# A routed MoE kernel: a late transfer on another queue, expert 0 in tiles of 416 and 384 tokens, and another order of copies and products at the end

## The chip, the cores and the metric

The kernel runs on one core of one Trainium2 chip. The core has five engines that run on their own and wait for each other by semaphores: TensorE (PE in the profile; PEld is its loading of weights), VectorE (DVE), ScalarE (ACT), GpSimd (POOL) and SyncE (SP), which here only issues transfers. The metric is device time in microseconds, the median over runs. The kernel before took 938.18 us (three runs, 937.0 to 938.84).

## The reference, cut to what matters

Two blocks follow each other. The first is attention with a polynomial sketch, over 4 batches, 4 heads, 1088 positions and 32 dimensions; its output becomes x, with one row for each of the 4352 tokens. The second routes every token to all 8 experts, with weights from 8 rounds of Sinkhorn scaling.

```
q_p, k_p = phi(q), phi(k)                 # phi: products of two projections, 64 features
num = q_p @ (k_p^T v);  den = q_p . sum(k_p) + 1e-6
x = (num / den), as (B*S, H*D) = (4352, 128)
P = exp(x @ w_gate - max)
8 times: P /= row sums; P /= column sums; P *= N / E
out = sum over e of P[:, e] * (relu(x @ w1[e]) @ w2[e])     # F = 1024
```

The column sums go over all tokens, so the routing can't begin before the last token's x is there. An expert's two products don't need the routing: only its weight in the sum does.

## The kernel before, in words

x is held transposed, as `xT`, 128 features by 4352 tokens. For each token the experts' products are by far the largest work. They are cut into groups, listed in `groups`: first token, tile width, number of tiles, experts, and whether the weights of the routing are multiplied into x first. While attention and routing still run, the plain groups are computed: expert 0 over all tokens but with its result stored unweighted in `kept`, and expert 1 over 1280 of them. The other groups are weighted, and take the experts that remain, on pieces of 256 tokens.

A plain group has two tiles. Its second product uses a scheme with seven products of half blocks in place of eight (`seven`), so VectorE forms differences of the relu outputs (L911, in `two`), and the sums come out in four PSUM banks. Each group goes through four blocks of four steps. A step is one first product with w1 (L894), its relu on ScalarE (L898), and second products (L1067) of a block that began eight steps earlier (`LAG`). When a group's banks are full, `part_of_seven` unloads them: ScalarE copies (L729 to L744) and VectorE adds (L720 and L723). The next group can write to a bank only when that bank has been read; bank 0 is free after L723 on `kept`, the fourth bank after L723 on `w`.

Attention and routing are written as generators (`attention`, `routing`) and are mixed with these steps by `fill(n)`: it advances the expert work by about n units, where a step with tiles of 480 tokens is one unit and a step with n tokens n/480. The order of TensorE and VectorE is thus written out by hand in this stretch; ScalarE's is set by a scheduler.

Attention of batches 1 to 3 runs in three thirds. For each, `tops` makes the products (L454), `over` divides and turns the result (L473), and `take_over` moves it into `xT` through DRAM: one transfer out (L478), then one for each of four heads (L480). For batch 3 this is done in two pieces, after the second and after the third third, both on GpSimd's queue. Once everything is there, `logits` multiplies x by w_gate (L488), VectorE turns the result (L497), and the Sinkhorn rounds alternate between VectorE (L587 to L603) and one small product on TensorE (L597). At the end the weights go to DRAM as `pT` (L609), and come back spread over partitions as `xe`, which GpSimd multiplies with x (L663).

The last group has two tiles of 256 tokens. Its last two blocks are written out with their products in an order of their own (`last_products`): of the last eight blocks, the products that go to bank 1 are held back and fill TensorE at the end, while the other three banks are unloaded. `last_part` does that: banks are finished in the order 3, 0, 2, 1, and copies (L772 to L782), adds (L764), transposes (L699) and stores (L852) follow.

Of the kernel before, what the change touches and what calls it, by code (L numbers as in the profile page):

```python
# [50 lines left out]
def kernel(  # L51
# [12 lines left out]
    nc = tc.nc  # L64
# [62 lines left out]
    W9 = 9 * 32  # L127
# [159 lines left out]
    def transpose_q(b, lo=0, hi=S):  # L287
        to = kT if b == 1 else qT
        nc.vector.transpose(out=to[:, lo:hi], in_=loaded["q", b].rearrange("p a d -> p (a d)")[:, lo:hi])
# [35 lines left out]
    def keys_sums(b):  # L325

        kp, vx = products.pop(b), v_slots[b % 2]
        pv = bank()[:, 0:128].rearrange("p (i c d) -> p i c d", i=2, c=2)

        slots = [slice(h, H + 1, H - h) for h in range(H)]  # L330

        for t in range(NT + 1):
            n = P if t < NT else 64
            for h in range(H):
                i, s = divmod(h, 2)
                nc.tensor.matmul(pv[64 * s:64 * (s + 1), i], kp[0:n, H * t + h].rearrange("p i j -> p (i j)"),  # L336
                                 vx[0:n, slots[h], t, :], start=(t == 0 and i == 0), stop=(t == NT and i == 1),
                                 tile_position=(0, 64 * s))
        sums_of[b] = pv
# [3 lines left out]
    def keys_kept(b):  # L343
        pv = sums_of.pop(b)
        for s in range(2):
            sl = slice(64 * s, 64 * (s + 1))
            if b:
                x, y = kvs[b % 2][sl, :, s, :], pv[sl].rearrange("p i c d -> p i (c d)")[:, :, 0:D + 1]
            else:
                x, y = kvz[sl, :, :, s, :], pv[sl].rearrange("p i c d -> p c i d")  # L350
            if s:
                nc.vector.tensor_copy(x, y)
            else:
                nc.scalar.copy(x, y)
# [55 lines left out]
    def queries_ab(b):  # L410
        qa = dram.tile([H * R, 2, 2, 2 * W9], F32, name=f"qa{b}")
        qb = dram.tile([2, R, 2 * R, 2, 2 * W9], F32, name=f"qb{b}")
        ab = wk.tile([P, 3, 192], F32, tag="qab", name="qab", bufs=1)
        x = (kT if b == 1 else qT).rearrange("p (h q c t s) -> p h c t q s", h=2, q=2, c=3, t=3)
        for cs in ((0, 1), (2,)):
            pq = bank()[:, 0:192 * len(cs)].rearrange("p (c n) -> p c n", n=192)
            for i, c in enumerate(cs):
                for s in range(2):
                    nc.tensor.matmul(pq[64 * s:64 * (s + 1), i].rearrange("p (t q s) -> p t q s", t=3, q=2),
                                     wdq.rearrange("p n f -> p (n f)"), x[:, s, c], start=True, stop=True,  # L420
                                     tile_position=(0, 64 * s))
            nc.scalar.copy(ab[:, cs[0]:cs[-1] + 1], pq)
        abf = ab.rearrange("p c n -> p (c n)")
        for s in range(2):
            x = abf[64 * s:64 * s + 32].unsqueeze(1).to_broadcast([32, 2, 2 * W9])
            nc.sync.dma_start(out=qa[:, :, s], in_=x)
        for s in range(2):
            for h in range(2):
                x = abf[64 * s + 32 + h:64 * (s + 1):2].unsqueeze(1).to_broadcast([2 * R, R, 2 * W9])
                nc.sync.dma_start(out=qb[h, :, :, s].rearrange("i f n -> f i n"), in_=x)  # L430
        queries[b] = qa, qb
# [11 lines left out]
    def times(b, c):  # L443
        ph = third(phs[b % 2], c)
        nc.vector.tensor_tensor(ph, ph, third(rb, c), op=Alu.mult)

    def tops(b, c):

        pn = bank()[:, 0:3 * H * (D + 1)].rearrange("p (t h d) -> p t h d", t=3, h=H)
        ph = third(phs[b % 2], c)  # L450
        for t in range(3):
            for i in range(2):
                for s in range(2):
                    nc.tensor.matmul(pn[64 * s:64 * (s + 1), t, 2 * i:2 * i + 2].rearrange("p h d -> p (h d)"),  # L454
                                     ph[:, i, s, 64 * t:64 * (t + 1)], kvs[b % 2][:, i].rearrange("p h d -> p (h d)"),
                                     start=(t == 0 and i == 0), stop=False, tile_position=(0, 64 * s))
        for s in range(2):
            nc.tensor.matmul(pn[64 * s:64 * (s + 1), :, :, D], ones[:, 0:64], eps, start=False, stop=True,
                             tile_position=(0, 64 * s))
        queries[b, c] = pn  # L460

    turned = {}
# [9 lines left out]
            turned[b] = wk.tile([P, H, W9], F32, tag="xt", name="xt", bufs=1)  # L472
        nc.vector.transpose(out=turned[b][:, :, 96 * c:96 * (c + 1)].rearrange("p h (t s) -> p h t s", t=3), in_=xs)  # L473

    def take_over(b, lo, hi):

        xd = dram.tile([P, H, hi - lo], F32, name=f"xd{b}{lo}")
        nc.gpsimd.dma_start(out=xd, in_=turned[b][:, :, lo:hi])  # L478
        for h in range(H):
            nc.gpsimd.dma_start(  # L480
                out=xT[32 * h:32 * (h + 1), b * S:b * S + 4 * W9].rearrange("d (f n) -> d f n", f=4)[:, :, lo:hi],
                in_=xd.rearrange("(f d) h n -> h d f n", f=4)[h])

# [15 lines left out]
    def attention(b):  # L499


        follows = b + 1 < B
        keys_sums(b)
        times(b, 0)
        yield
        keys_kept(b)
        times(b, 1)
        tops(b, 0)
        if b == 1:
            transpose_q(2)  # L510
        yield
        times(b, 2)
        if b == 1:
            queries_ab(2)
            repeat_a(2)
        if follows:
            repeat_b(b + 1)
        over(b, 0)
        tops(b, 1)
        yield  # L520
        over(b, 1)
        if b + 1 == B:
            take_over(b, 0, 192)
        yield
        tops(b, 2)
        if follows:
            transpose_k(b + 1)
        if b + 2 < B:
            load_k(b + 2)
            load_v(b + 2)  # L530
        yield
        over(b, 2)
        if b + 1 < B:
            take_over(b, 0, W9)
        else:
            take_over(b, 192, W9)
        if follows:
            keys_ab(b + 1)
            yield
            keys_products(b + 1, 0)  # L540
            if b == 1:
                transpose_q(3)
            yield
            keys_products(b + 1, 1)
            if b == 1:
                queries_ab(3)
                repeat_a(3)
            yield
            keys_products(b + 1, 2)
            yield  # L550
# [11 lines left out]
    def routing():  # L562
# [45 lines left out]
        for b in (1, 0, 2, 3):  # L608
# [8 lines left out]
    lower, upper = slice(0, H2), slice(H2, P)  # L617
# [3 lines left out]


    groups = [(0, 256, 2, [0], False), (512, 288, 2, [0], False), (0, 256, 2, [1], False),
              *((1088 + 960 * i, 480, 2, [0], False) for i in range(3)), (3968, 192, 2, [0], False),
              (512, 384, 2, [1], False)]
    PLAIN = len(groups)
    for lo in (1280, 512, 2048, 2816, 3584):
# [83 lines left out]
    def room(tag, n=NMAX):  # L711
        return keep.tile([P, NMAX], F32, tag=tag, name=tag)[:, 0:n]
# [44 lines left out]
    def last_part(g, k):  # L757


        lo, n, *_ = groups[g]  # L760
        s0, s1, s2, s3 = sums[g]

        def add(out, a, b):
            nc.vector.tensor_tensor(out, a, b, op=Alu.add)  # L764

        own = parts.setdefault(g, {})
        if not own:
            own.update(y=[pools[0].tile([P, NT3], F32, name=f"y{t}", bufs=1)[:, 0:n] for t in range(2)],
                       **{a: room(a, n) for a in "zwxfr"})
        (y1, y2), z, w, x, f, r = (own[a] for a in "yzwxfr")  # L770
        if k == 3:
            nc.scalar.copy(r[upper], s3[lower])  # L772
            add(w[upper], s3[upper], r[upper])
        elif k == 0:
            nc.scalar.copy(z[upper], s0[lower])
            nc.scalar.copy(f[lower], s0[upper])
            add(x[upper], z[upper], w[upper])
            add(z[upper], x[upper], s0[upper])
            add(z[lower], s0[lower], f[lower])
            nc.scalar.copy(x[lower], s0[lower])  # L780
        elif k == 2:
            nc.scalar.copy(r[lower], s2[upper])  # L782
            add(y2[upper], z[upper], s2[upper])
            add(z[lower], z[lower], s2[lower])
            add(y2[lower], z[lower], r[lower])
            add(x[upper], x[upper], s2[upper])
            put(y2, lo + n, n, (nc.sync, nc.scalar))
        else:
            add(y1, s1, x)
            put(y1, lo, n, (nc.sync, nc.scalar))  # L790
# [220 lines left out]
    held = []  # L1011

    def last_products():

        k = len(blocks) - 2
        one, two_ = ([[(b, p) for p in ps] for ps in seven(b)] for b in (k, k + 1))
        return one + held[:3] + two_ + held[3:]

    def kept_to_sums(g):

# [205 lines left out]
```

## Time and profile before

| what | us |
| --- | --- |
| median of three runs | 938.18 |
| span of the profiled execution | 933.0 |
| TensorE busy | 914.5 |
| VectorE busy | 693.6 |
| ScalarE busy | 416.9 |
| GpSimd busy | 206.2 |
| TensorE's longest single wait (before L488) | 2.5 |
| first product with routing's weights (L894 on xe) | at 197.92 |
| TensorE's last product ends | at 926.2 |

The span is that of one execution under the profiler, and is a little shorter than the timed runs. A line of the timeline has the start in us from the span's beginning, the length in us, the engine, the line of the kernel, the operation, what it writes and reads, and in brackets how long the engine had been idle before it and what ended that. A matmul of the program appears as two records in the trace, and two of them run side by side on the two halves of the columns. Records overlap, so the pace is read from the distances of their starts.

### The profile page before, as it was taken

Reading aid. Unit: us, or ns where it says so; the run is one execution under the profiler, and the core shown is the slowest. Engines: PE = TensorE matmul, PEld = TensorE weight load, DVE = VectorE, ACT = ScalarE, POOL = GpSimd, SP = SyncE. Lnnn points to the kernel's source line nnn. Section 1 sums busy time; section 2 is a strip of 40 time slices with the busy share of each in tenths; the row PEclk is TensorE's granted clock in tenths of the full one; section 3 lists DMA queues with packets and bytes.
Section 4 is the critical chain, followed back from the end, with each engine's and each line's share of the span. In section 5 each row is a group of like instructions: output and inputs, shape, how many; then the busy total and the mean of one; then the engine's idle time right before and its main releaser. Section 6 shows DMA issues by size and latency. Waiting matters only on the chain.

```text
span 933.0 us, 18870 instructions
## 1 busy us (share of the span) xinstructions
PE 914.5 (98%) x7434; PEld 588.2 (63%) x7434; DVE 693.6 (74%) x1200; ACT 416.9 (45%) x901; POOL 206.2 (22%) x203
## 2 busy tenths in 40 slices
PE   8999899999999999999999999999999999999997
PEld 6666546656666666666666666666666666667885
DVE  8788579887778778585976666965757977768655
ACT  2444345554444454444544444544445444445443
POOL 2011200091655501130020101101110343311210
PEclk9999999999999999999999999999999999999999
DMA  8987100222335545354353534363434556542640
GB/s 229 290 248 214 52 1 1 64 95 81 107 123 168 184 127 162 110 186 131 121 151 132 168 111 145 111 185 128 146 110 152 153 148 196 165 171 91 180 143 12
DMA packets 90728, 128.14 MB, mean 137 GB/s; under 512 B 24352, under 2 KB 68464, under 8 KB 85904
## 3 DMA queue, kind: packets, MB, share of 16 engines
q1 hardware_dynamic: 88240, 123.24, 43.0%
q0 software_dynamic: 1168, 3.54, 1.3%
q8 instruction: 58, 0.95, 0.4%
q10 hardware_dynamic: 1232, 0.16, 0.1%
q14 instruction: 30, 0.25, 0.1%
HBM read 107.88 MB, written 19.05 MB: 136 GB/s over the span
## 4 chain that ended last, share of the span: by engine, by line
PE 88%; DVE 6%; DMA 2%; issue 2%; ACT 1%; POOL 1%; SPq 0%; DVEq 0%; ACTq 0%; POOLq 0%
PE a L894 46%; PE s L1067 39%; DVE hb L911 1%; DMA xd<-xt 1%; POOL xT L480 1%; PE a L336 1%; DMA kx<-in_k_dram 0%; PE a L384 0%; DVE kT L293 0%; DMA ph<-qa 0%; DVE cs L593 0%; PE a L454 0%; PE s L366 0%; DVE kp L320 0%; DVE rs L587 0%
## 5 line engine op out<-in xcount | busy, mean ns | idle before, releaser
L894 PE MATMUL a<-xe,w 128*64 128x256 f32 (+1 forms) x2560 | 525.8, 470 | 0.0
L898 ACT ACTIVATE hb<-a 128x256 f32<-128x256 f32 (+5 forms) x408 | 195.2, 480 | 256.1 <-PE a L894 225.8
L898 ACT ACTIVATE hx<-a 128x256 f32<-128x256 f32 (+1 forms) x360 | 167.2, 465 | 213.4 <-PE a L894 193.8
L894 PEld LDWEIGHTS a<-xe,w 128*64 128x64 f32 x2560 | 220.4, 137 | 65.2 <-issue 1.3
L1067 PE MATMUL s<-hb,ws 128*64 128x256 f32 (+4 forms) x1344 | 241.1, 395 | 1.0 <-DVE hb L911 1.0
L1067 PE MATMUL s<-hx,ws 128*64 128x256 f32 x1280 | 208.7, 379 | 0.2 <-DVE kept L723 0.2
L956 DVE TENSOR_TENSOR hx<-hx 128x512 f32<-128x512 f32 (+1 forms) x204 | 150.1, 745 | 71.2 <-ACT hx L898 66.1
L956 DVE TENSOR_TENSOR hb<-hb 128x512 f32<-128x512 f32 (+1 forms) x204 | 131.0, 653 | 93.4 <-ACT hb L898 89.5
L663 POOL TENSOR_TENSOR xe<-xT,xe 128x768 f32<-128x768 f32 (+2 forms) x41 | 84.0, 2049 | 499.8 <-DMA xe<-pT 474.1
L1067 PEld LDWEIGHTS s<-hb,ws 128*64 128x64 f32 x1344 | 119.6, 137 | 101.9 <-issue 73.7
L1067 PEld LDWEIGHTS s<-hx,ws 128*64 128x64 f32 x1280 | 112.7, 137 | 91.1 <-issue 70.5
L894 PE MATMUL a<-xT,w 128*64 128x480 f32 (+4 forms) x512 | 122.5, 464 | 1.1 <-DVE rd L469 0.9
L1067 PE MATMUL s<-hb,w 128*64 128x256 f32 (+4 forms) x496 | 103.4, 411 | 1.8 <-DVE kept L723 1.8
L911 DVE TENSOR_TENSOR hb<-hb 128x480 f32<-128x480 f32 (+8 forms) x96 | 65.6, 685 | 17.4 <-ACT hb L898 10.2
L1067 PE MATMUL s<-hx,w 128*64 128x256 f32 x384 | 69.3, 379 | 0.0
L894 PEld LDWEIGHTS a<-xT,w 128*64 128x64 f32 x512 | 52.0, 137 | 25.3 <-issue 10.9
L1067 PEld LDWEIGHTS s<-hb,w 128*64 128x64 f32 x496 | 47.8, 137 | 24.2 <-issue 6.5
L239 POOL TENSOR_TENSOR ws<-w 128x256 f32<-128x256 f32 (+1 forms) x70 | 60.0, 893 | 12.7 <-PE a L894 8.2
L911 DVE TENSOR_TENSOR hx<-hx 128x256 f32<-128x256 f32 (+1 forms) x65 | 38.8, 603 | 24.5 <-ACT hx L898 23.4
L956 DVE TENSOR_TENSOR pqg<-hb 128x512 f32<-128x512 f32 x68 | 48.3, 751 | 0.0
L1067 PEld LDWEIGHTS s<-hx,w 128*64 128x64 f32 x384 | 35.9, 137 | 8.6
L956 DVE TENSOR_TENSOR pqg<-hx 128x512 f32<-128x512 f32 x68 | 36.6, 578 | 0.0
(170 smaller groups left out, 480.9 us busy)
## 6 DMA issues: line engine op xcount, KB each, us to landing
w<-in_moe_w_dram SPq DMA_DIRECT2D x82, 512.0 KB, 5.4
ws<-ws SPq DMA_DIRECT2D x34, 1024.0 KB, 4.9
xe<-pT SPq DMA_DIRECT2D x34, 384.0 KB, 4.0
ws<-ws SPq DMA_DIRECT2D x12, 512.0 KB, 3.8
qb<-qab SPq DMA_DIRECT2D x12, 288.0 KB, 4.2
ph<-qa SPq DMA_DIRECT2D x12, 288.0 KB, 5.1
rb<-qb SPq DMA_DIRECT2D x3, 1152.0 KB, 8.2
pb<-pT SPq DMA_DIRECT2D x6, 384.0 KB, 6.7
```

Of the source, the lines that this page charges most:

```text
L239: tc.keep_in_program_order(nc.gpsimd.tensor_tensor(ws[:, c:c + len(ns)], blocks(x), blocks(y), op=Alu.subtract if off else Alu.add))
L336: nc.tensor.matmul(pv[64 * s:64 * (s + 1), i], kp[0:n, H * t + h].rearrange("p i j -> p (i j)"), vx[0:n, slots[h], t, :], start=(t == 0 an ...
L480: nc.gpsimd.dma_start(out=xT[32 * h:32 * (h + 1), b * S:b * S + 4 * W9].rearrange("d (f n) -> d f n", f=4)[:, :, lo:hi], in_=xd.rearrange( ...
L663: tc.keep_in_program_order(nc.gpsimd.tensor_tensor(out, x, pb, op=Alu.mult))
L894: nc.tensor.matmul(ph[sl], loaded_w[j][0][:, P * f + H2 * s:P * f + H2 * (s + 1)], sources[j][:, lo:hi], start=True, stop=True, tile_posit ...
L898: nc.scalar.activation(out=out, in_=ph, func=Act.Relu)
L911: nc.vector.tensor_tensor(out, a, b, op=Alu.subtract)
L956: nc.vector.tensor_tensor(out if not isinstance(out, tuple) else places(*out), places(*a), places(*b) if isinstance(b, tuple) else b, op=A ...
L1067: nc.tensor.matmul(sums[g][i][H2 * s:H2 * (s + 1), n * place:n * (place + 1)], w, x, start=c == 1, stop=c == per, tile_position=(0, H2 * s))
```

## The change

It has three parts. The second piece of batch 3's x goes through SyncE's queue instead of GpSimd's. Expert 0's plain groups over tokens 1088 to 4351 were three of 2 x 480 and one of 2 x 192; they become three of 2 x 416 and one of 2 x 384. At the end, the copy of bank 0's lower half into x is issued right after the two other copies of that bank, so that the next copy doesn't queue behind it, and one of the held-back pairs of products is moved from before the last block's products to behind them, so that the other banks finish earlier.

```diff
-    def take_over(b, lo, hi):
+    def take_over(b, lo, hi, queue):
         xd = dram.tile([P, H, hi - lo], F32, name=f"xd{b}{lo}")
-        nc.gpsimd.dma_start(out=xd, in_=turned[b][:, :, lo:hi])
+        queue.dma_start(out=xd, in_=turned[b][:, :, lo:hi])
         for h in range(H):
-            nc.gpsimd.dma_start(
+            queue.dma_start(
...
         if b + 1 == B:
-            take_over(b, 0, 192)
+            take_over(b, 0, 192, nc.gpsimd)
...
         if b + 1 < B:
-            take_over(b, 0, W9)
+            take_over(b, 0, W9, nc.gpsimd)
         else:
-            take_over(b, 192, W9)
+            take_over(b, 192, W9, nc.sync)
...
     groups = [(0, 256, 2, [0], False), (512, 288, 2, [0], False), (0, 256, 2, [1], False),
-              *((1088 + 960 * i, 480, 2, [0], False) for i in range(3)), (3968, 192, 2, [0], False),
+              *((1088 + 832 * i, 416, 2, [0], False) for i in range(3)), (3584, 384, 2, [0], False),
               (512, 384, 2, [1], False)]
...
         elif k == 0:
             nc.scalar.copy(z[upper], s0[lower])
             nc.scalar.copy(f[lower], s0[upper])
+            nc.scalar.copy(x[lower], s0[lower])
             add(x[upper], z[upper], w[upper])
             add(z[upper], x[upper], s0[upper])
             add(z[lower], s0[lower], f[lower])
-            nc.scalar.copy(x[lower], s0[lower])
...
-        return one + held[:3] + two_ + held[3:]
+        return one + held[:2] + two_ + held[2:]
```

## The prediction

> **What bounds the kernel now.** I read the busy shares first, then the waits of the matmul engine, then the timeline around each long wait, then the end.
>
> ```profile
> PE 914.5 (98%) x7434; PEld 588.2 (63%) x7434; DVE 693.6 (74%) x1200; ACT 416.9 (45%) x901; POOL 206.2 (22%) x203
> ```
>
> TensorE never has much to spare, so I also read the starts of its records. Four 480-wide records start 0.81 us after the four before (0.20 each), four 192-wide ones 0.32 us after (0.08 each). The ratio is 2.5 = 480/192: TensorE pays by the column at both widths. Laying all of the program's columns end to end at this pace gives about 890 us; the other 43 us of the 933.0 us span are start, waits and end. Only those can be won. The waits of TensorE, with total, count and longest in us:
>
> ```profile
> PE a L488 <- issue: 2.5, 1, 2.5
> PE s L1067 <- DVE kept L723: 2.1, 3, 1.6
> PE s L1067 <- DVE hb L911: 1.0, 2, 0.7
> ```
>
> L488 is the logits product, which needs all of x. The timeline of GpSimd and TensorE there (start, length) shows why it waits:
>
> ```profile
> 102.11 0.72 POOL L478 DMA_DIRECT2D xd<-xt  x1 [11.99 <-DVE xt L473]
> 104.23 0.58 DVE L473 STREAM_TRANSPOSE xt<-rd 128x384 f32<-128x384 f32 x1
> 106.14 2.20 POOL L480 DMA_DIRECT2D xT<-xd  x4 [3.31 <-DMA xd<-xt]
> 108.33 0.76 POOL L478 DMA_DIRECT2D xd<-xt  x1
> 111.25 2.20 POOL L480 DMA_DIRECT2D xT<-xd  x4 [2.16 <-DMA xd<-xt]
> 112.07 0.85 PE L488 MATMUL a<-xT,wg 128*32 128x384 f32 x6
> 115.42 1.99 PE L488 MATMUL a<-xT,wg 128*32 128x384 f32 x18 [2.50 <-issue]
> ```
>
> The last third of batch 3's x is turned by 104.8, but its transfer is issued at 108.33, behind the four issues of the earlier part. The other two waits lie in the routing stretch. The table by stage (length, then busy us of PE, PEld, DVE, ACT, POOL) shows VectorE near full there:
>
> ```profile
> 118.00:176.00 58.00, 55.66 (x328) 32.55 (x326) 50.61 (x94) 30.28 (x58) 0.00 (x0) 1.00 0.00 1
> ```
>
> After 920 the chain is VectorE's. ScalarE's copy at L780 stands ahead of L782, which VectorE needs:
>
> ```profile
> 925.15 0.42 DVE L764 TENSOR_TENSOR z<-s,f 64x256 f32<-64x256 f32 x1
> 925.60 0.37 ACT L780 COPY x<-s 64x256 f32<-64x256 f32 x1 [1.17 <-DVE z L764]
> 925.99 0.37 ACT L782 COPY r<-s 64x256 f32<-64x256 f32 x1
> 926.39 0.42 DVE L764 TENSOR_TENSOR y<-z,s 64x256 f32<-64x256 f32 x1 [0.82 <-ACT r L782]
> ```
>
> [...]
>
> **Part 1, the late piece of x on SyncE.** SyncE's queue, by its own timeline:
>
> ```profile
> 77.42 0.46 SPq L438 DMA_DIRECT2D rb<-qb  x1
> 176.82 1.42 SPq L609 DMA_DIRECT2D pT<-qT  x4
> ```
>
> It issues nothing between 77.9 and 176.8 us, so nothing is queued behind its new wait and nobody waits for it. Worked out: ready 104.8; issue about 0.6 (its L426 issues: 1.23 for two); landing 2.6 (GpSimd's 192 KB row) to 3.5, so 108.0 to 108.9; four issues of about 0.5, 2.0; landing 2.1, so the last lands at 112.1 to 113.0. TensorE has work at L488 until 112.9. The 2.5 us wait falls to 0 to 0.5. Saved: 2.0 to 2.5, I take 2.5, since the new tile sizes put 0.9 us more of other products ahead of the logits. If 384-byte pieces made each issue take 1 us (the trace has up to 1.24 for L430), it would save 0.5 to 1.
>
> **Part 2, tiles of 416 and 384.** 3 x 960 + 384 = 3 x 832 + 768 = 3264 columns, with the same number of instructions: TensorE's own time does not change, nor does the amount of padding. What changes is the moment at which one group's sums are unloaded, against attention and routing. I went through the order of instructions on each engine at four places.
>
> (a) Products of batch 3's attention (L454, now 93.23, no wait). Before, VectorE's copy L352 and products L445 stand ahead of the next block's subtraction L911. In the new order L911 comes first, and it waits for the relu of the first product after L336. Counting from the end of L336: relu done 1.7 (as at 91.14 to 92.84 now), L911 1.0, L723 0.4, L352 0.25: 3.4. TensorE, with fewer columns ahead, is there at 2.3. New wait: 1.1, between 0.6 and 1.4.
>
> (b) The first group's unload. Before, it fell after the logits, and the next group's L1067 waited 1.6 (1.96 lost by starts) for L723. Now its sums are added around the logits and that wait goes. But L723 on w, on which the next group's fourth bank waits, stands behind the first routing iteration. From the end of L488: maximum product done 4.3, L578 and L579 to 4.95, the exponential waits behind ScalarE's unload copies to 6.5, L584 to L593 2.5 to 9.05, L911 1.0, L723 0.5: 10.5. TensorE arrives at 9.1. New wait about 1.4.
>
> (c) The second group's unload. An iteration from L600 to L593 takes 2.8 (143.00 to 145.77), a block's L911 0.95 + 1.15 with overlap. TensorE's interval between two L597 is now 5.2 at first (6.0 before), and VectorE comes out about 1.1 us behind at each. In the new order L723 on bank 0 comes after the whole fourth iteration and a pair of L911: 23.85 + 2.8 + 1.1 + 0.55 + 0.55 = 28.9 after the logits. TensorE wants that bank at 27.3. New wait about 1.7; before, the same place cost nothing (153.87).
>
> (d) The 192-wide group. TensorE ran through it so fast that it met VectorE's 480-wide work: 0.99 lost at 170.1 and about 0.4 in slips of 0.2 near it. At 384, steps last twice as long: saved 1.4.
>
> Sum of part 2: +1.1 - 2.0 + 1.4 + 1.7 - 1.4 = +0.8. VectorE is busy 87% of this stretch, so each wait may be off by about 0.7; together I allow -1.2 to +2.8. Afterwards the additions of the last group are twice as wide while GpSimd works. [...] (192-wide adds take 0.36, but 0.88 at 191.16 to 192.96). I count some 1 to 1.5 us more of VectorE work there, hidden under 24 us of products. xe is weighed from 186.3 and used at 197.9, so routing has 10 us in hand and stays off the path.
>
> **Part 3, the end.** One pair of products (4 records of 0.108) goes behind the products of the last block: banks 3, 0 and 2 finish 0.43 earlier. The subtraction needed by p7 is done at 921.7, and p7 would start at 922.2, so it doesn't wait. Moving L780 up takes its 0.37 and its wait out: the 0.82 hole before 926.39 closes. VectorE's eleven operations, from 923.64 to 929.59, then end near 928.4, and the stores follow. TensorE's end at 926.2 is unchanged and not the limit, as the last add starts at about 927.5. Saved: 0.43 + 0.8 = 1.2, between 0.8 and 1.3.
>
> **Sum.** -2.5 + 0.8 - 1.2 = -2.9; 938.2 - 2.9 = 935.3 us.
>
> **Rivals.** First, VectorE keeps up better than I count, (b) and (c) cost nothing: -2.5 + 1.1 - 2.0 - 1.4 - 1.2 = -6.0 at most; with half of (b) and (c) left, -4.5, so 933.7. For it: before, the second unload cost nothing. Against: its place in the order has moved behind an iteration. Second, VectorE falls further behind at the shorter intervals, and the waits take back the logits' gain: only the end and some of the rest stay, -0.8, 937.4. For it: 87% busy. Against it: the sum of VectorE's work is no larger. Third, slower: x's transfers on SyncE are slow (1 us an issue and 1 us more to land), which leaves 2 us of the logits wait, and part 2 costs 2.8 and an extra 1 us under GpSimd: -0.5 + 3.8 - 1.2 = +2.1, 940.3. Against: SyncE's queue is idle then, and two of the three parts can't lose.
>
> **How the numbers follow.** The forecast 0.42, the first rival 0.26, the second 0.23, the third 0.09. The forecast and the first rival lie below 936.3 (0.2%), with a little of them and nearly all of the second within it: faster 0.67, the same 0.25, slower 0.08. The range, 932.7 to 938.0, takes in the first rival but for its far end (932.2), and the second; what lies outside is the third and the tails.
>
> **What would show it.** Right: L488 in one run of 24 records of 2.9 us with no wait; SyncE issuing L478 and L480 around 105 to 112; a wait of about 1.1 before the L454 near 94; waits on L723 of 1 to 2 us near 126 and 145; no wait near 170; ScalarE's last two copies before VectorE asks, the last transpose 1.2 us nearer to TensorE's last product. Wrong: a wait left at L488, waits in routing that add up to under 1 or over 5 us, or a first product of xe that waits for GpSimd.

## The result, and the profile after

The changed kernel takes 931.25 us (median of 4 runs, 930.81 to 931.37), the kernel before 937.86 in the same comparison (937.0 to 938.84): a ratio of 0.9928, 95% interval 0.9911 to 0.9946, so 6.6 us less. The forecast was 2.9 less, with 5.5 at the far end of its range.

The first reading of the two profiles already shows something odd: they differ by 933.0 - 929.5 = 3.5 us of span, about half of what the timed runs differ by. The profiled execution of the kernel before took 934.94 us, 2.1 less than any of its timed runs so far; the prediction took its waits from this execution and its starting point from the others. What those runs had that this one lacked is the main subject of the experiments.

The busy shares of the changed kernel are those of before, to 1%:

```profile
PE 915.1 (98%) x7434; PEld 596.6 (64%) x7434; DVE 696.7 (75%) x1200; ACT 417.5 (45%) x901; POOL 204.3 (22%) x198
```

Of TensorE's waits (what waits, on what; total, count, longest), L488 is gone from the list; those in the routing stretch are shorter, and one before L454 is new:

```profile
PE s L1067 <- DVE w L723: 0.9, 1, 0.9
...
PE a L454 <- issue: 0.6, 1, 0.6
...
PE s L1067 <- DVE hb L956: 0.6, 1, 0.6
PE s L1067 <- DVE kept L723: 0.4, 1, 0.4
...
PE s L1067 <- DVE hb L911: 0.3, 1, 0.3
```

The timeline around the logits (start, length) shows the two pieces of x on two queues. The late piece leaves at 106.43, where it left at 108.33 before, and its four last transfers start at 109.45 instead of 111.25. TensorE comes to L488 later too, at 113.96 instead of 112.07, and does all 24 records in one run:

```profile
101.97 0.72 POOL L478 DMA_DIRECT2D xd<-xt  x1 [10.96 <-DVE xt L473]
105.24 2.20 POOL L480 DMA_DIRECT2D xT<-xd  x4 [2.56 <-DMA xd<-xt]
106.43 0.57 SPq L478 DMA_DIRECT2D xd<-xt  x1
109.45 1.74 SPq L480 DMA_DIRECT2D xT<-xd  x4
113.96 2.04 PE L488 MATMUL a<-xT,wg 128*32 128x384 f32 x24
```

The table by stage for the routing stretch: TensorE is busy 56.62 of 58 us where it had 55.66, while VectorE has more to do than before (52.12 against 50.61):

```profile
118.00:176.00 58.00, 56.62 (x355) 29.28 (x353) 52.12 (x99) 30.73 (x63) 0.00 (x0) 1.00 0.02 3
```

At the end ScalarE's last two copies are done before VectorE asks. The hole of 0.82 is closed, and VectorE's adds follow at 0.45 us each. The copy that was moved up (now L777) takes back a little: the first add shown waits for it, and starts 0.68 us after the one before it instead of 0.53:

```profile
921.44 0.37 ACT L777 COPY x<-s 64x256 f32<-64x256 f32 x1
921.83 0.37 ACT L782 COPY r<-s 64x256 f32<-64x256 f32 x1
921.84 0.42 DVE L764 TENSOR_TENSOR z<-x,s 64x256 f32<-64x256 f32 x1 [0.25 <-ACT x L777]
922.29 0.42 DVE L764 TENSOR_TENSOR z<-s,f 64x256 f32<-64x256 f32 x1
922.74 0.42 DVE L764 TENSOR_TENSOR y<-z,s 64x256 f32<-64x256 f32 x1
...
925.48 0.45 DVE L699 STREAM_TRANSPOSE yt<-y 128x256 f32<-128x256 f32 x1
```

### The profile page after: what moved, and what is told of

Same layout as the page of the kernel before. It is cut to its first block, busy times and chain, and to the rows that moved or that the text cites. A ratio compares the mean times of both kernels' runs of the same rounds, so it can differ in the third digit from the quotient of the medians.

```text
span 929.5 us, 18877 instructions
## 1 busy us (share of the span) xinstructions
PE 915.1 (98%) x7434; PEld 596.6 (64%) x7434; DVE 696.7 (75%) x1200; ACT 417.5 (45%) x901; POOL 204.3 (22%) x198
## 4 chain that ended last, share of the span: by engine, by line
PE 91%; DVE 6%; issue 1%; ACT 1%; DMA 0%; SPq 0%; POOL 0%; DVEq 0%; ACTq 0%; POOLq 0%
PE a L894 49%; PE s L1067 39%; DVE hb L911 1%; PE a L336 1%; PE a L114 1%; DVE hb L956 1%; PE a L454 1%; DMA ph<-qa 0%; PE a L304 0%; ACT hb L898 0%; DVE cs L593 0%; DVE kp L320 0%; DVE kT L293 0%; DVE pqg L956 0%; PE a L488 0%
## 5 line engine op out<-in xcount | busy, mean ns | idle before, releaser
L894 PE MATMUL a<-xe,w 128*64 128x256 f32 (+1 forms) x2560 | 571.3, 470 | 0.0
L898 ACT ACTIVATE hb<-a 128x256 f32<-128x256 f32 (+4 forms) x408 | 195.3, 480 | 253.4 <-PE a L894 226.3
L894 PEld LDWEIGHTS a<-xe,w 128*64 128x64 f32 x2560 | 242.7, 137 | 76.6 <-issue 1.6
L1067 PE MATMUL s<-hb,ws 128*64 128x256 f32 (+3 forms) x1344 | 267.5, 395 | 1.8 <-DVE w L723 0.9
L1067 PE MATMUL s<-hx,ws 128*64 128x256 f32 x1280 | 235.4, 379 | 0.0
L1067 PEld LDWEIGHTS s<-hb,ws 128*64 128x64 f32 x1344 | 127.8, 137 | 92.7 <-issue 63.8
L1067 PEld LDWEIGHTS s<-hx,ws 128*64 128x64 f32 x1280 | 121.2, 137 | 78.7 <-issue 59.4
L894 PE MATMUL a<-xT,w 128*64 128x416 f32 (+3 forms) x512 | 124.4, 464 | 1.3 <-DVE rd L469 0.9
L1067 PE MATMUL s<-hb,w 128*64 128x256 f32 (+3 forms) x496 | 109.6, 410 | 0.5 <-DVE kept L723 0.4
L911 DVE TENSOR_TENSOR hb<-hb 128x416 f32<-128x416 f32 (+7 forms) x96 | 68.1, 711 | 18.2 <-ACT hb L898 12.9
L1067 PE MATMUL s<-hx,w 128*64 128x256 f32 x384 | 76.5, 379 | 0.0
L1067 PEld LDWEIGHTS s<-hb,w 128*64 128x64 f32 x496 | 50.0, 137 | 23.2 <-issue 6.8
L911 DVE TENSOR_TENSOR hx<-hx 128x256 f32<-128x256 f32 (+1 forms) x65 | 38.8, 602 | 24.6 <-ACT hx L898 20.8
L1067 PEld LDWEIGHTS s<-hx,w 128*64 128x64 f32 x384 | 38.6, 137 | 8.5
```

The lines of the kernel that those rows point to most:

```text
L894: nc.tensor.matmul(ph[sl], loaded_w[j][0][:, P * f + H2 * s:P * f + H2 * (s + 1)], sources[j][:, lo:hi], start=True, stop=True, tile_posit ...
L898: nc.scalar.activation(out=out, in_=ph, func=Act.Relu)
L911: nc.vector.tensor_tensor(out, a, b, op=Alu.subtract)
L1067: nc.tensor.matmul(sums[g][i][H2 * s:H2 * (s + 1), n * place:n * (place + 1)], w, x, start=c == 1, stop=c == per, tile_position=(0, H2 * s))
```

## The experiments

Ratios are to the kernel before on the same chip; in us they are taken of 937.05, the median of its 64 timed runs in all these comparisons. As that kernel varies, a ratio is not quite the quotient of two medians. By the medians of all runs on the same chip, the queue alone makes 3.6 us, the tiles alone 4.6, both together 5.2 and the change without the queue 5.4, where the ratios below give 4.9, 5.3, 5.1 and 6.4. Two numbers are used throughout. *Lost by starts* is the distance from one TensorE start to the next, less the record's columns at 2.4 per ns (480 columns in the 0.20 us from one 480-wide start to the next), added over a stretch. The *mean granted clock* of TensorE is listed for every timed run.

### Each part alone, and all but the queue

Three theories stood at this point. A: the piece of x on GpSimd's queue is often later than in the first profile, so the missing 3 us lie at L488. B: they lie in the routing stretch and come with the tiles. C: they are a difference between two occasions on which the kernel before was measured.

**Queue only.**

```diff
-            take_over(b, 192, W9)
+            take_over(b, 192, W9, nc.sync)
```

> Only the late piece of x goes to SyncE's queue; tiles and end as before. The two profiles account for 3.5 us, the timed runs differ by 6.6; some 3 us are missing. Theory A (the piece on GpSimd's queue is often later than in the profiled execution of before, and the missing time lies in the wait at L488): 4.5 to 6 us faster than before. Theory B (the missing time lies in routing, where VectorE is nearly full, and comes with the tiles): 2.5 to 3 us faster, what the profile of before shows as the wait. Theory C (the missing time is a difference between occasions of measuring before, and no effect of the change): 2.5 to 3 us.

Measured: 933.39 us, ratio 0.9948 (0.9932 to 0.9965), 4.9 us less (3.3 to 6.4). That is more than the 2.5 us that the wait at L488 had in the first profile, as theory A said. The waits in the routing stretch stayed as they were.

**Tiles only.**

```diff
-              *((1088 + 960 * i, 480, 2, [0], False) for i in range(3)), (3968, 192, 2, [0], False),
+              *((1088 + 832 * i, 416, 2, [0], False) for i in range(3)), (3584, 384, 2, [0], False),
```

> Only the tiles of 416 and 384; queue and end as before. By the profile of after, the tiles save about 0.8 us (the waits near 126 and 170 go, smaller ones near 94, 125 and 144 come). Theory A: 0.5 to 1 us faster. Theory B: 3 to 4 us faster. Theory C: 0.5 to 1 us. My prediction as it was made: 0.8 us slower.

Measured: 932.37 us, ratio 0.9943 (0.9927 to 0.9959), 5.3 us less (3.8 to 6.8). Theory B comes nearest with 3 to 4; A and C had said 0.5 to 1. The surprise is in the timeline. The late piece is still on GpSimd's queue, and yet L488 doesn't wait:

```profile
106.86 0.75 POOL L478 DMA_DIRECT2D xd<-xt  x1
109.74 2.19 POOL L480 DMA_DIRECT2D xT<-xd  x4 [2.13 <-DMA xd<-xt]
113.38 2.35 PE L488 MATMUL a<-xT,wg 128*32 128x384 f32 x24
```

TensorE arrives 113.38 - 112.07 = 1.31 us later than before, and the last transfers start 111.25 - 109.74 = 1.51 earlier, as VectorE turned the second third of x sooner, so that the first piece left at 101.39 instead of 102.11, and this piece landed sooner (2.57 us after its issue instead of 3.31). Together 2.8 us: the new order closes the wait from both sides.

**End only.**

```diff
-        return one + held[:3] + two_ + held[3:]
+        return one + held[:2] + two_ + held[2:]
```

and the copy at L780 moved up, as in the change.

> Only the other order of copies and products at the end. All theories: 1.0 to 1.2 us faster, with the last transpose some 2.3 us after TensorE's last product, in place of 3.4.

Measured: 935.96 us, ratio 0.9990 (0.9981 to 0.9999), 0.9 us less (0.1 to 1.8). The time from TensorE's last start to the end of the span is 6.07 us, against 7.12: 1.05 less, as planned.

**The change without the queue.** The changed kernel with `nc.gpsimd` in the last call of `take_over`.

> The changed kernel with the late piece of x back on GpSimd's queue. Theory A: only 1.5 to 2 us faster than before, so the queue is worth 4.5 or more. Theory B: 4 us faster than before. Theory C: about 1.5 to 2 us faster, and the queue alone 2.5 to 3, the two of them adding up to 4 to 5.

Measured: 931.54 us, ratio 0.9932 (0.9915 to 0.9949), against 0.9928 with the queue. None of the theories had this kernel so fast (at most 4 us less were expected, 6.4 came). Once the tiles are there, the queue's worth can't be told from nothing by these intervals; in the profiles L488 takes 2.45 us without it and 1.97 with it, as batch 3's products come a little late.

### Why the kernel before varies by 7 us

Its 64 timed runs went from 933.96 to 940.99 us, while the whole change's ten stayed between 930.13 and 931.85. So it was profiled again.

> The kernel before once more, one profile. Theory S (the profile that the prediction was read from, 934.94 us, was of a quick execution, some 2 us better than the median of 936.9 to 937.9): this one comes at 935.7 or more, again with a wait of 2.5 to 3.5 us at L488, and beside it waits of 0.5 to 1 us near 189 and near 410 to 415 that the first profile lacks. Rival (that profile was typical, and the 2 us are lost in no place that a profile shows): the same waits as before to within 0.2 us each, whatever the time.

Measured: 940.04 us, span 938.1, with a wait of 3.19 at L488. The other waits that were expected did not come: near 189 and 410 there is none over 0.4. The timeline of this second profile of the kernel before, and under it its table by stage (length, busy us of PE, PEld, DVE, ACT, POOL, then the granted clock):

```profile
114.53 0.85 PE L488 MATMUL a<-xT,wg 128*32 128x384 f32 x6
118.56 3.32 PE L488 MATMUL a<-xT,wg 128*32 128x384 f32 x18 [3.19 <-DMA xT<-xd]
```

```profile
114.90:118.50 3.60, 0.47 (x6) 0.00 (x0) 0.00 (x0) 0.00 (x0) 1.67 (x4) 0.91 0.24 55
118.50:121.80 3.30, 3.24 (x18) 1.01 (x18) 1.13 (x2) 0.00 (x0) 0.00 (x0) 0.58 0.00 0
121.80:128.00 6.20, 6.20 (x35) 2.83 (x36) 2.59 (x5) 2.82 (x5) 0.00 (x0) 1.00 0.00 0
```

In the 3.3 us after the wait the granted clock is 0.58 on average (0.79 over the 8 us from 114 to 122). The same eighteen records of L488 took 1.99 us in the first profile, after a wait of 2.50. In the profile of the end alone they took 1.99 after a wait of 2.95, at full clock:

```profile
112.59 0.85 PE L488 MATMUL a<-xT,wg 128*32 128x384 f32 x6
116.39 1.99 PE L488 MATMUL a<-xT,wg 128*32 128x384 f32 x18 [2.95 <-DMA xT<-xd]
```

So a wait can cost more than itself: after 3.19 us of it the eighteen records took 3.32 - 1.99 = 1.33 us more.

The length of the wait alone does not decide it. The clock fell 2.46 us into this wait, and 2.83 us into the one of the next experiment, but stayed full through all 2.95 us of the wait in the profile of the end alone. In all 14 profiles the clock changes only at points that are whole multiples of 3.413 us apart: in the second profile it is full for 112.640 us, half for 3.413, full for 812.372 (33, 1 and 238 times as long); in the first it is full for 925.012 (271 times), up to the half clock at the end. When the execution is cut into periods at these points, each of the 16 full-clock periods with TensorE busy for 1.12 us or less is followed by half clock (14 of them at the program's end), and each of the more than 3700 others, with 1.68 us or more, by full clock. The waits at L488, with the last row from the experiment that follows:

| kernel | wait | periods (us) | TensorE busy in each | granted clock in each |
| --- | --- | --- | --- | --- |
| before, first profile | 2.50 | 110.46 to 113.87, to 117.28 | 2.46, 1.86 | 1.00, 1.00 |
| end only | 2.95 | 111.24 to 114.66, to 118.07 | 2.20, 1.68 | 1.00, 1.00 |
| before, second profile | 3.19 | 114.43 to 117.84, to 121.25 | 0.94, 2.69 | 1.00, 0.50 |
| wait made longer | 4.27 | 112.55 to 115.96, to 119.37, to 122.79 | 0.58, 1.97, 3.42 | 1.00, 0.50, 0.50 |

In the first two the wait lies across the end of a period; in the other two most of it lies in one. An estimate from these bounds (2.29 us idle in a period were enough, 1.73 were not): a wait of 2.50 that falls anywhere on the periods is followed by half clock in four to seven of ten runs, without being any longer. How many of the runs owe their half clock to this, and how many to a longer wait, isn't shown.

Of the 938.1 - 933.0 = 5.1 us between the two profiles of the kernel before, the stretch at L488 makes 2.0; the first 50 us, while the inputs arrive, make 1.9 (more lost by starts), the stretches before and after the logits 0.5 each.

**The wait made longer.** GpSimd copies the late piece twice into spare memory ahead of its L478; the kernel before is otherwise unchanged.

```diff
     def take_over(b, lo, hi):
-
+        for i in range(2 if b + 1 == B and lo else 0): nc.gpsimd.dma_start(out=dram.tile([P, H, hi - lo], F32, name=f"xe{i}"), in_=turned[b][:, :, lo:hi])
```

> The kernel before, with the wait at L488 made longer: GpSimd copies the late piece twice into spare memory that nobody reads, ahead of its L478, at about 0.76 us an issue, so the piece comes 1.5 us later. Theory K (a wait of TensorE over about 3 us drops the granted clock for the next few us: 18 records of L488 took 3.32 us at a granted 0.79 after the wait of 3.19, against 1.99 at 1.00 after waits of 2.50 and 2.95): the wait is 4.0 to 4.7, the 18 records after it take 3 us or more, and every timed run has a mean clock of 0.997 or less. Rival (the slow records of that one profile were chance): the wait is the same 4.0 to 4.7, the records take 2.0, and the clocks spread from 0.996 to 0.999 as in the kernel before. In both the time rises by about 1.5 us over the kernel before; theory K adds about 0.6 more, for the runs of before that had been spared.

Measured: 940.58 us, ratio 1.0040 (1.0024 to 1.0057), 3.7 us more. All eight timed runs have a mean clock of 0.994 or 0.995, as theory K said and its rival did not. The timeline, and under it the table by stage:

```profile
112.29 0.85 PE L488 MATMUL a<-xT,wg 128*32 128x384 f32 x6
117.40 3.81 PE L488 MATMUL a<-xT,wg 128*32 128x384 f32 x18 [4.27 <-DMA xT<-xd]
```

```profile
117.40:122.80 5.40, 5.40 (x24) 1.53 (x25) 2.12 (x4) 0.00 (x0) 0.00 (x0) 0.50 0.00 0
122.80:128.00 5.20, 5.20 (x32) 2.41 (x30) 1.60 (x3) 2.68 (x5) 0.00 (x0) 1.00 0.00 0
```

Half clock, for 5.4 us after the wait this time. The expectation of about 2.1 us more was too small; it counted on the shorter stretch of half clock of the profile above.

The mean clocks of the timed runs tell about how often this happens to the kernel before. They also hold the half clock after the program's last products, 0.7 to 4.5 us in these profiles. With the end as before, this alone leaves a mean of 0.998 or more, and one period of half clock besides it brings 0.997 or less; with the shorter end it can also leave 0.998:

| kernel | runs | mean clock 0.997 or less | median of these | median of the others |
| --- | --- | --- | --- | --- |
| before | 64 | 35 | 938.01 | 935.76 |
| wait made longer | 8 | 8 | 940.58 | none |
| end only | 22 | 10 | 936.55 | 934.92 |
| queue only | 5 | 1 | 933.47 | 933.12 |
| tiles only; tiles and end; queue and tiles | 17 | 0 | | |
| the whole change (both sets) | 10 | 0 | | |

The kernels that keep the wait, before and the end alone, have such runs in about half of the cases. The one run of the queue alone took no longer than its others, and may be a long half clock at its end. The ten runs of the whole change lie within 1.7 us, with no second group.

The first profile's execution, at a mean clock of 0.998 and 934.94 us, was like the 29 that were spared, and quick among them.

Of the first three theories, A has the place right for much of the missing time: it lies at L488, in part as clock and in part as products out of step (below), and not as a wait alone. C falls, as the medians of the kernel before on three occasions were 936.94, 937.72 and 936.85. B is left for the next two kernels.

**The wait made shorter.** Routing starts one unit later (6, as shown), then two units later (7); queue, tiles and end as before.

```diff
     def routing():
 
-        yield 5
+        yield 6
```

> The kernel before, with routing one unit later (two units took the wait away entirely): one pair of pairs of 480-wide products more stands ahead of L488, 1.6 us, so a wait of 0.9 to 1.6 us is left. Theory K: no wait of 3 us is left, so the records at L488 take 2.0 and nearly every timed run has a mean clock of 0.998 or more; time 1.6 us less by the shorter wait and 0.7 by the clock, 2.3 in all, if the routing stretch gives nothing back. Rival (the clock of a run has nothing to do with this wait): clocks of 0.996 and 0.997 in half of the runs, at most 1.6 less.

> The kernel before with one number changed: routing starts two units later, so four more pairs of 480-wide products stand ahead of the logits. Neither queue nor tiles are changed. Theory W (what the queue and the tiles each take away is the one wait at L488 and what it drags along; anything that brings TensorE there 2 to 4 us later does it): no wait at L488, 3.0 to 4.5 us less than before, so 932.4 to 933.9, and highest minus lowest under 3 us as in the other kernels without this wait. Rival T (the tiles gain by their own shape in the routing stretch, and only 2.5 us by the wait): 1 to 2.5 us less, 934.4 to 935.9, as waits on L723 remain or new ones come, since every unload meets another place of routing.

Measured, one unit: 935.99 us, ratio 0.9990 (0.9978 to 1.0002), mean clock 0.998 or more in all 14 runs. Two units: 934.68, ratio 0.9964 (0.9950 to 0.9979), and 10 of 11 runs. The clock went as theory K had it. The time did not: at one unit 2.3 less was expected, and 0.9 came. In both profiles L488 no longer waits, though batch 3 is still out of step and L488 takes 2.7 us; the routing stretch gives some back. Lost by starts between the logits and the first product on xe: 6.69 and 6.38, against 5.54 and 6.08 in the two profiles of before; a wait of 1.03 before L1067 near 181 is new. The rest of the miss at one unit, about 1 us, isn't found in its one profile, where the first piece landed in 2.56 us (3.31 and 3.98 in the profiles of before). A slower landing may bring back some of the wait in other runs, but no profile showed it. At two units, the runs spread over 5.2 us, where theory W had expected under 3; one of them, at 937.91, has a mean clock of 0.997.

So theory W holds in its main point: moving routing takes away what the queue takes away. Against it, the tiles alone did better (5.3 us) than two units (3.4). These intervals overlap, but the profiles show a gain of the tiles' own in routing: 4.31 lost by starts there, against 6.38 with two units.

### Do the parts add up?

Queue and tiles together, the end as before:

> Queue and tiles together, the end as before. If their gains added up, 3.5 + 4.6 = 8.1 less than before: 928.8. Theory W (they are substitutes for the same wait): about as the tiles alone, 4.6 to 5.0 less, 931.9 to 932.4. If the queue still does harm or good of its own on top of the tiles, it shows as the difference to 932.4. The end then is worth this time minus the whole change's 931.25: 0.7 to 1.1 expected.

Measured: 932.48 us, ratio 0.9946 (0.9930 to 0.9962), 5.1 us less. The queue alone had 4.9, the tiles alone 5.3. They are two ways to remove one wait. The end, on top of both, brings it to the 0.9928 and 0.9939 of the whole change. This was run once more beside its variants:

> The changed kernel once more, on the same chip and against the same runs of before as its variants. Theory K: no wait of 3 us, mean clocks of 0.998 or more in all runs, 931.0 to 931.5, all runs within 2.7 us. Rival: the tight 0.6 us of its first four runs was chance, and it spreads as widely as the kernel before, over 4 us.

Measured: 930.76 us (930.13 to 931.85), ratio 0.9939 (0.9921 to 0.9956). The spread is 1.7 us; its rival had expected over 4.

### Can the remaining waits in routing go?

First, one unit more before the product of the maximum, so that VectorE does L723 on w ahead of the first iteration:

```diff
-        yield 2
+        yield 3
         pm = bank()[:, 0:P]
```

> The changed kernel with one number changed: routing's product of the maximum comes one unit (two pairs of 416-wide products) later, so VectorE does the subtraction and L723 on w ahead of the first iteration, and L723 on kept ahead of the fourth. Theory V (the two waits on L723, 0.94 near 126 and 0.44 near 145, are VectorE's order and no more): both go, nothing new comes, routing ends some 1.7 us later with nobody waiting: 931.3 - 1.3 to 1.7 = 929.6 to 930.0. Rival (VectorE is the bound of this stretch and the waits only move): within 0.4 of 931.3, with waits of 0.4 to 1 us at other places between 120 and 176. Third: the weights of xe come too late and TensorE waits near 195 for GpSimd, 1 us or more, 931.5 to 932.5.

Measured: 930.72 us, ratio 0.9930 (0.9913 to 0.9947). The waits near 126 and 145 are gone. In their place TensorE loses 0.65 before a column sum near 134, and 1.08 before another group's unload:

```profile
165.36 0.54 PE L1067 MATMUL s<-hb,w 128*64 128x384 f32 x1 [0.75 <-DVE kept L723]
```

The stretch from the logits to xe loses 3.99 instead of 4.32: of the 2.1 us that the two waits cost by starts, 0.3 stay saved. VectorE, 52 of 58 us busy, moves the waits and doesn't end them. The rival is right in its mechanism here; the time, expected within 0.4 of 931.3, is 0.2 below that.

Then, with this, batch 3's L352 and L445 ahead of L911:

```diff
-        yield
-        keys_kept(b)
-        times(b, 1)
+        if b + 1 < B: yield
+        keys_kept(b); times(b, 1)
+        if b + 1 == B: yield
```

> The changed kernel with routing's product of the maximum one unit later, and with batch 3's copy L352 and its products L445 moved ahead of the next block's subtraction L911 on VectorE. Theory V (the 0.91 lost before L454 near 94 is VectorE's order and no more): it goes, 930.7 - 0.9 = 929.8. Rival (the 1.2 us of L352 and L445 come back as a later L911 or L723): a wait of 0.5 to 1 us at L1067 near 96 to 98 in its place, 930.5 to 931.0.

Measured: 930.31 us (928.78 to 932.11), ratio 0.9934 (0.9915 to 0.9953), beside 930.76 for the change on the same chip. In its profile the 0.91 before L454 is gone and nothing takes its place: from 50 us to the logits 7.47 is lost by starts, against 8.39 to 8.53. Both variants' medians are a little lower than the change's, but their runs overlap with its runs, so neither is shown to beat it. The 930.31 lies between what theory V (929.8) and its rival (930.5 to 931.0) had expected.

## Why the prediction was wrong

Here is the loss by starts of each stretch, with L488 as the time from its first start to the next product's, and the end as the time from TensorE's last start to the end of the span:

| stretch | before, first profile | before, second | tiles only | the change, first profile | the change, second |
| --- | --- | --- | --- | --- | --- |
| 0 to 50 us | 12.46 | 14.40 | 12.22 | 12.75 | 12.65 |
| 50 us to L488 | 7.86 | 8.38 | 8.48 | 8.53 | 8.39 |
| L488 | 5.26 | 7.28 | 2.28 | 1.97 | 1.97 |
| to the first product on xe | 5.54 | 6.08 | 4.31 | 4.32 | 4.31 |
| products on xe | 7.60 | 7.69 | 7.88 | 8.60 | 7.64 |
| end | 7.12 | 7.14 | 7.11 | 6.22 | 6.20 |

The direction was right, and so was each place that the prediction named; its size was less than half of the measured one.

**"The 2.5 us wait falls to 0 to 0.5. Saved: 2.0 to 2.5, I take 2.5": the step that failed, mis-sized.** The stretch at L488 fell by 3.3 us against the first profile and by 5.3 against the second. Two things were missing from the term. The first is the clock: after the wait it falls to one half, by the mean clocks in 35 of 64 runs, and those runs are 2.25 us longer. The prediction read a wait of 2.50 in an execution with full clock, and didn't ask whether other executions looked the same, though x's landing sets the length of the wait and varies (2.56 to 3.98 us for the first piece in these profiles), and so does the place of the wait on the periods of 3.413 us. The second is the shape of L488. The four batches' products start 0.007 us apart in the changed kernel's records and run side by side, 0.30 to 0.35 for each chunk's four. When batch 3's x is missing, the other three start without it, and 24 records take 0.85 + 1.99 = 2.84 us of work in place of 2.04. So 2.5 of wait and 0.8 of lost pairing make up the 3.3.

**"938.2 - 2.9".** The terms came from an execution of 934.94 us and were taken off a median of 938.18. From the execution itself the sum gives 932.0; the change's profile has 931.37. That this is so near is in part luck: the first and the fifth stretch of the table happened to be 1.3 us worse in the change's profile. The 3.2 us between the two starting points were in the numbers at hand, and no step of the prediction explained them. In the later runs they come apart: the three runs lay 1.1 above the median of 64, the runs at a lower clock lift that median by 1.3 over the others', and the profiled execution was 0.8 quicker than those.

**"since the new tile sizes put 0.9 us more of other products ahead of the logits".** The products were 0.9 us, as counted. But TensorE came to L488 1.3 us later in the tiles alone, as it had lost 0.4 more by starts on the way, and the last transfers started 1.5 us earlier as well. The prediction booked this under the queue. With the tiles, the queue was hardly needed: 0.9932 without it, 0.9928 with it. This booking left the sum alone, as the wait can be taken away only once, but it gave the credit to the wrong part.

**Part 2, "+0.8".** In the table it is -0.5 against the first profile, +0.7 before the logits and -1.2 after them, and -1.6 against the second. (a) lost 0.91 by starts at L454, where 1.1 was counted, and 0.2 came back around it. (b) went as said, for the reason given: the old wait of 1.96 left, and L723 on w brought 1.28, with 1.4 counted. (c) was mis-sized, 0.78 for 1.7 (28.9 - 27.3, its own figures, is 1.6). VectorE was done with L723 when the prediction said, 28.8 us after the logits; but TensorE asked about 0.8 us later than counted. The likely reason is the 1.28 that it had lost before: a wait moves the engine that waits, so later waits on the same partner shrink. No run separates this from other causes. (d) went as said: nothing is lost near 170. The lengths counted for VectorE at the new widths, such as 1.0 for L911 in (a) and (b), were the author's estimates; in the changed kernel's profile L911 takes 0.59 on average at 416 columns and 1.02 at 832, against 0.65 and 1.15 at 480 and 960. The 1 to 1.5 us more of VectorE work while GpSimd works was an estimate too. Three adds that it counts on, L720 of expert 0's last group, don't show it: at 384 columns they take 0.81, 0.81 and 0.72 (189.31 to 192.31), where they took 0.88, 0.88 and 0.79 at 192. That GpSimd's work is what lengthens an add was not shown.

**Part 3, "-1.2".** It measured 0.9 to 1.1 in the spans, and 0.9 (0.1 to 1.8) alone. Right; 0.15 was lost again to the new wait for L777.

**Sum.** Against the first profile, -3.3 - 0.5 - 0.9 = -4.7. About 2 us more in 35 of 64 runs add 1.1 on average: -5.8. The two comparisons measured -6.7 and -5.7 (0.9928 and 0.9939). Between the profiles in this table, the stretch before 50 us differs by up to 2.2 us, and the one after the first product on xe by 1.0. That is more than what is left over, so that remainder is not assigned.

**Rivals and signs.** The first rival, that VectorE keeps up better, was nearest in its mechanism (half of (c) gone) and in its number (933.7); the 932.2 at its far end was still too high. Of the signs, those that were to show it wrong did not appear: no wait is left at L488, the waits in routing lie between 1 and 5 us, and xe doesn't wait for GpSimd. They tested the mechanism. None tested the starting point.

## What to carry to other kernels

When the profiled execution is quicker than the timed runs by as much as the gain in question, find what varies first: a second profile, and the clock of each run beside its time, would have shown it. Here a TensorE wait of 2.95 us was not followed by half clock, and one of 3.19 was; the first lay across the end of a period of 3.413 us, the second mostly in one. By the length of the half clock after it, that cost about 1.3 us more at 3.19, and 2.7 at 4.27. So the runs of one kernel split into two groups, and removing the wait is worth more than its length in one profile. When two parts of a change act ahead of the same wait, book the wait once and test each part without the other.

## What the runs showed of the hardware

- TensorE ran at full clock after waits of 2.50 and 2.95 us. With waits of 3.19 and 4.27 it ran at half clock for one and two periods of 3.413 us, the first of which began within the wait.
- The clock changed only at points that are whole multiples of 3.413 us apart. In all 14 profiles a full-clock period with TensorE busy for 1.12 us or less was followed by half clock, and one with 1.68 or more by full clock. What lies between the two figures is not known.
- Four products with 32 output partitions each, started 0.007 us apart, took 0.30 to 0.35 us together. One batch out of step cost 0.8 us in 24 records.
- From SyncE's queue the late piece's four issues took 1.74 us, against 2.20 from GpSimd's (0.43 and 0.55 each); the first transfer's issue took 0.57 against 0.76.
